# Pooled attention into a two-layer MLP: the output product of four more groups in seven products of quarters, and one set of raw tiles

## The chip, the cores and the metric

The kernel runs on one core of one Trainium2 chip. Its time is the device time of one execution in microseconds (us). The kernel before took 300.4 us, the median of three runs (300.05 to 300.6). Engines are named as the profile names them: PE (matrix products; PEld its weight loads), DVE (vector), ACT (scalar), POOL (GpSimd), SP (here only a queue that issues DMAs).

## The reference

The inputs are q, k, v of shape 8 batches x 8 heads x 576 rows x 64, and two weight matrices, 512 x 2048 and 2048 x 512. The output is 4608 x 512 in float32.

```
k_p = k.reshape(B, H, Sp, 8, D).mean(axis=3)      # 72 pooled keys per head
v_p = v.reshape(B, H, Sp, 8, D).mean(axis=3)
scores = scale * np.matmul(q, k_p.transpose(0, 1, 3, 2))
attn = softmax(scores)                            # over the 72 pooled keys
x = np.matmul(attn, v_p).transpose(0, 2, 1, 3).reshape(B * S, H * D)
h = x @ w_in
g = h - np.tanh(h)
out = g @ w_out
```

## The kernel before, in words

**Groups.** The 4608 tokens are nine groups of 512. Groups 0 to 7 hold the first 512 rows of one batch each; group 8 holds the last 64 rows of all eight batches (the tails, two batches to a unit). A loop over g runs the MLP of group g while it prepares the attention of batch nb = g + 1 and the operands of batch nb + 1 = g + 2. There is no planner: each engine runs its instructions in the order in which the program emits them, and dictionaries (`plan`, `PLAN7`) say after which step of the MLP each step of attention is emitted.

**First product (lines 979 to 998).** `h_mms` makes 128 hidden rows for 512 tokens with 4 matmuls (L426), 64 in all for 16 rows of blocks. For each pair `h_act` runs tanh on ACT (L439) and subtracts on DVE (L440) into `gT`, 16 blocks x 512 tokens in bf16.

**Output product, ordinary (lines 1030 to 1052, groups 1 to 5).** `o_mms` (L483) makes 128 tokens x 512 columns with 16 matmuls, 64 for the group, in 16 steps u.

**Output product, in seven (lines 999 to 1029, groups 6 to 8, `SEVEN`).** A scheme of Winograd's kind with two output column halves, two halves of the 2048 hidden rows and two token halves: seven products (`PRODUCTS`, in the order 4, 2, 7, 1, 6, 5, 3) of 16 matmuls with 256 columns (L561), so 14 steps u and 112 matmuls, and sums round them. `w_sums` (L526) makes four weight sums T1 to T4 once, eight DVE operations. `g_sum` (L543) makes S1 to S4 from quarters of gT in each group: S3 in two halves after steps 13 and 15 of the first product, S2 after u = 2, S1 on POOL behind S2, S4 after u = 8. The products accumulate on top of one another in PSUM banks; `evacuate` copies or subtracts after each (ACT, some DVE), `finish_11` and `finish_22` add the parts on POOL (L593, L594, L598), `store_half` writes the result out.

**Where the sums lie.** T1 to T4 lie in k_raw[0] and v_raw[0], S1 and S2 in q_raw[0], S3 and S4 in q_raw[1], and three partial results n0, n1, p2 in k_raw[1]. So groups 2 to 5, which load batches into both sets of raw tiles, do not use the seven products.

**Attention of batch nb.** Four blocks of 128 rows, and for some groups a tail unit: scores on PE (`s_mms`, L292), row maximum and shift on DVE (L304, L307), exp on ACT (L343), a DMA transpose of E for two blocks at a time (`e_turn_dma`, L352), values on PE (`av_mms`, L379), reciprocal and scaling on DVE (L400, L401), a DMA transpose into xT (`x_turn_dma`, L409), which is what the next group's first product reads.

**Operands.** v of batch nb is pooled on POOL at the start of group g (`pool_v`, L224 to L237). q of batch nb + 1 is cast on ACT behind steps 13 and 15 of the first product (L261) and transposed by DMA; its k is pooled on POOL (`pool_k`, L209 to L215), transposed by DMA (L253) and placed by POOL (L247). Raw tiles exist twice (index b % 2). `load_for(g)` emits the loads of v for batch g + 1 and of q and k for batch g + 2 near the end of a group (u = 13). All these loads, the transposes and the stores are issued from SP, in order; an entry that waits holds back everything behind it.

**Tail values.** In groups of `SEVEN`, the values of a tail unit (`tail_values`) and its transpose are put into `carry` and emitted in the next group after steps 3 and 5 of its first product.

## Time and profile before

| what | value |
|---|---|
| median of three runs | 300.4 us |
| the profiled execution: its own time, and its span | 301.8 us, 300.1 us |
| mean granted PE clock | 0.991 |
| HBM read, written | 36.70 MB, 9.44 MB |
| DVE, tanh subtraction L440 | 64 in all, 1,219 ns each |
| POOL, first step of v's and k's pooling (L224, L209) | 2,908 ns each |
| POOL waiting for v (L224) | 35.7 us in 6 places |
| PE matmul, 512 columns and 256 columns, as recorded | 379 ns and 272 to 273 ns |

Matmuls are pipelined, so their recorded durations overlap; the distance from one to the next is what counts. A row of a timeline is: start in us from the beginning of the span, duration in us, engine, line, operation, what it writes and reads, shapes, how many. In the chain of work a row is start, duration, engine, line and how many. Groups of the kernel are told apart by the times at which the first matmul of L426 starts.

### The profile page before, as it was taken

To read this page: it belongs to the slowest core of one execution; us is meant where nothing else is said; L and a number is where in the kernel's file an instruction comes from. 1 tells how busy PE (TensorE), PEld (TensorE's weight loads), DVE (VectorE), ACT (ScalarE), POOL (GpSimd) and SP (SyncE) were. 2 spreads that over 40 slices of the span, in tenths; PEclk is the share of its full clock that TensorE was granted. 3 is DMA by queue.
4 is the path that set the end of the run, shared out by engine and by line. 5 is a ranking of instruction groups with operands and counts; after the bars stand their busy time and mean duration, and the time that the engine had idled before them with its cause. 6 is when DMAs were issued, how large, how long until landed. Compare 5 with 4: busy or idle time off the path is not lost.

```text
span 300.1 us, 5150 instructions
## 1 busy us (share of the span) xinstructions
PE 286.5 (95%) x2011; PEld 167.5 (56%) x2027; DVE 206.2 (69%) x292; ACT 142.9 (48%) x200; POOL 121.7 (41%) x111
## 2 busy tenths in 40 slices
PE   6799799999999999999999999999999999999993
PEld 2489765444554455445544554455447854784582
DVE  6786484878835993398339932986699947945772
ACT  1786255158504851476137623672376345505620
POOL 7846906029610791098107910791063830010000
PEclk9999799999999999999999999999999999999998
DMA  7999996699988999886889798959823540011005
GB/s 233 225 283 272 205 264 172 129 262 314 228 219 212 332 151 217 239 298 114 204 248 312 137 185 257 328 73 214 232 68 69 103 167 17 2 70 73 0 3 140
DMA packets 84377, 54.55 MB, mean 182 GB/s; under 512 B 58976, under 2 KB 72416, under 8 KB 84352
## 3 DMA queue, kind: packets, MB, share of 16 engines
q1 hardware_dynamic: 77552, 44.90, 57.8%
q0 software_dynamic: 6416, 8.91, 14.3%
q10 hardware_dynamic: 384, 0.39, 0.5%
q8 instruction: 16, 0.26, 0.4%
q14 instruction: 9, 0.07, 0.1%
HBM read 36.70 MB, written 9.44 MB: 154 GB/s over the span
## 4 chain that ended last, share of the span: by engine, by line
PE 77%; DVE 8%; DMA 7%; POOL 3%; ACT 2%; issue 1%; SPq 0%; ACTq 0%; POOLq 0%; DVEq 0%
PE PS L426 32%; PE PS L483 26%; PE PS L561 11%; DMA k_raw<-in_k_dram 4%; PE PS L379 4%; DVE gT L440 3%; DMA q_raw<-in_q_dram 3%; PE PS L292 2%; DVE sh L307 2%; DVE mx L304 2%; PE PS L446 1%; POOL k_raw L209 1%; ACT t_sb L439 1%; PE PS L273 1%; POOL k_raw L212 1%
## 5 line engine op out<-in xcount | busy, mean ns | idle before, releaser
L440 DVE TENSOR_TENSOR gT<-PS,t_sb 128x1024 bf16<-128x1024 f32 x64 | 77.0, 1219 | 40.2 <-ACT t_sb L439 40.2
L426 PE MATMUL PS<-xT,w1b 128*128 128x512 bf16 x448 | 100.8, 379 | 0.0
L483 PE MATMUL PS<-w2b,gT 128*128 128x512 bf16 x368 | 88.7, 379 | 0.8
L439 ACT ACTIVATE t_sb<-PS 128x1024 f32<-128x1024 f32 x64 | 65.5, 1024 | 48.4 <-PE PS L426 47.0
L426 PEld LDWEIGHTS <-w1b 128*128 128x128 bf16 x512 | 49.4, 98 | 55.8
L483 PEld LDWEIGHTS <-gT 128*128 128x128 bf16 x384 | 35.3, 98 | 36.8
L505 ACT COPY o_h<-PS 128x512 f32<-128x512 f32 x22 | 12.8, 583 | 47.7 <-PE PS L483 44.0
L224 POOL TENSOR_TENSOR v_raw<-v_raw 128x1280 f32<-128x1280 f32 x6 | 17.4, 2908 | 35.7 <-DMA v_raw<-in_v_dram 35.7
L343 ACT ACTIVATE E<-sh 128x576 bf16<-128x576 f32 x31 | 21.2, 682 | 15.9 <-DVE sh L307 15.9
L307 DVE TENSOR_TENSOR sh<-PS,mx 128x576 f32<-128x576 f32 x35 | 26.5, 757 | 1.2
L304 DVE TENSOR_REDUCE mx<-PS 128x8 f32<-128x576 f32 x35 | 26.2, 748 | 1.5 <-PE PS L292 1.5
L400 DVE RECIPROCAL rden<-PS 128x8 f32<-128x8 f32 x36 | 7.4, 205 | 25.4 <-PE PS L379 23.4
L401 DVE TENSOR_TENSOR x_sb<-PS,rden 128x512 bf16<-128x512 f32 x32 | 22.1, 692 | 1.1
L561 PEld LDWEIGHTS <-q_raw 128*128 128x128 bf16 x192 | 18.5, 98 | 2.9 <-DVE q_raw L543 0.4
L247 POOL COPY KB<-kT 64x288 bf16<-64x288 bf16 x12 | 5.1, 421 | 35.6 <-DMA kT<-kd 30.2
L209 POOL TENSOR_TENSOR k_raw<-k_raw 128x1280 f32<-128x1280 f32 x6 | 17.4, 2908 | 0.0
L446 PE MATMUL PS<-xT,w1b 128*128 128x128 bf16 x256 | 17.2, 230 | 0.0
L446 PEld LDWEIGHTS <-w1b 128*128 128x128 bf16 x256 | 16.2, 104 | 0.0
L379 PEld LDWEIGHTS <-ET 128*128 128x128 bf16 x192 | 13.1, 98 | 5.2 <-ACT ET L362 0.8
L379 PE MATMUL PS<-VB,ET 128*128 128x130 bf16 (+2 forms) x192 | 15.8, 221 | 0.1
L561 PEld LDWEIGHTS <-gT 128*128 128x128 bf16 x144 | 13.9, 98 | 2.0
L292 PEld LDWEIGHTS <-qT 128*128 128x128 bf16 x128 | 10.0, 98 | 7.6 <-issue 0.8
(99 smaller groups left out, 290.7 us busy)
## 6 DMA issues: line engine op xcount, KB each, us to landing
k_raw<-in_k_dram SPq DMA_DIRECT2D x14, 512.0 KB, 8.6
q_raw<-in_q_dram SPq DMA_DIRECT2D x12, 512.0 KB, 6.9
v_raw<-in_v_dram SPq DMA_DIRECT2D x12, 512.0 KB, 5.1
out_dram<-o_h SPq DMA_DIRECT2D x24, 256.0 KB, 2.5
w1b<-in_moe_w_in_dram POOLq DMA_DIRECT2D x4, 512.0 KB, 9.0
q_raw<-in_q_dram POOLq DMA_DIRECT2D x2, 1024.0 KB, 14.2
w2b<-in_moe_w_out_dram POOLq DMA_DIRECT2D x4, 512.0 KB, 16.4
out_dram<-o_h SPq DMA_DIRECT2D x4, 512.0 KB, 3.3
```

What stands on the lines that cost most here:

```text
L209: eng.tensor_tensor(out=r[:, :, 0:4, :], in0=r[:, :, 0:4, :], in1=r[:, :, 4:8, :], op=ALU.add)
L304: nc.vector.reduce_max(out=mx.rearrange("p k h o -> p k (h o)"), in_=sc, axis=AX.X)
L307: nc.vector.tensor_tensor(out=sh[:, :, :, :], in0=sc, in1=mx.to_broadcast([128, 2, 4, G]), op=ALU.subtract)
L343: nc.scalar.activation(out=E[:, e, :, :].rearrange("p t c -> p (t c)")[:, 0:NK], in_=sh.rearrange("p k h c -> p (k h c)"), func=ACT.Exp, s ...
L379: nc.tensor.matmul(PS[ps, banks[half], D1 * h : D1 * (h + s1 - s0)], lhsT=ET[:, t, c0 : c0 + (ps.stop - ps.start)], rhs=VB[kb][:, t, s0:s1 ...
L401: nc.vector.tensor_tensor(out=x_sb, in0=ps[:, :, :, 0:D], in1=rden.to_broadcast([128, 2, 4, D]), op=ALU.mult,)
L426: nc.tensor.matmul(PS[:, bank, :].rearrange("p (j c) -> p j c", j=R), lhsT=w1b[:, fb, i * 128 : (i + 1) * 128], rhs=xT_of(g)[:, :, fb, :], ...
L439: nc.scalar.activation(out=t_sb[:, :, :], in_=ps, func=ACT.Tanh)
L440: nc.vector.tensor_sub(out=gT[:, i : i + 2, :], in0=ps, in1=t_sb[:, :, :])
L446: mm = nc.tensor.matmul(PS[:, bank, 128 * n : 128 * n + 128], lhsT=w1b[:, fb, (4 * c + n) * 128 : (4 * c + n + 1) * 128], rhs=xT_of(0)[:, ...
L483: mm = nc.tensor.matmul(PS[:, bank, 0 : c1 - c0], lhsT=gT[:, i, tb * 128 : (tb + 1) * 128], rhs=w2b[:, i, c0:c1], start=(i == 0), stop=(i ...
L561: nc.tensor.matmul(ps, lhsT=A[:, i, 128 * b : 128 * b + 128], rhs=B_[:, i, :], start=(n in "24" and i == 0), stop=(i == NQ - 1), skip_grou ...
```

## The change

The seven products are used in groups 2 to 8. T1 to T4 move to k_raw[1] and v_raw[1], S3, n0 and n1 to q_raw[1], p2 to k_raw[1]; S2 gets a tile of its own; S1 overwrites the quarter gT[HI, C2] and S4 the quarter gT[LO, C1]. Batches 2 to 7 use raw set 0 only. In groups of the seven products `pool_k` is emitted right behind `pool_v` at the start of the group, v of batch nb + 1 is loaded right behind the first product, and q's transpose, k's transpose with the tail's load, and the placing of k with the tail's cast and the next loads of q and k are emitted after u = 0, 7 and 13. The carried tail values come after u = 9 and 10 of a group that still has attention. The four weight sums are made in group 1 (their place is "the group before the first of `SEVEN`"). In group 1 v is loaded after u = 0 and 4, k's transpose comes after u = 10 instead of 4, and the stores after u = 4, 11 and 15.

```
-SEVEN = (6, 7, 8)
+SEVEN = (2, 3, 4, 5, 6, 7, 8)
...
+    T1, T2 = quarters(k_raw[1].rearrange("p t n -> p (t n)").bitcast(BF16))
+    T3, T4 = quarters(v_raw[1].rearrange("p t n -> p (t n)").bitcast(BF16))
+    S3 = quarters(q_raw[1].rearrange("p h j d -> p (h j d)").bitcast(BF16))[0]
+    S2 = const.tile([128, NQ, HC], BF16, name="S2")
+    n0, n1 = [
+        q_raw[1][:, h : h + 2, :, :].rearrange("p (b h) j d -> p b (h j d)", b=2) for h in (4, 6)
+    ]
+    p2 = k_raw[1][:, 4, :].rearrange("p (b c) -> p b c", b=2)
+
+    def raw_of(b):
+        return 1 if b == 1 else 0
...
-            1: (S1, a21, a22, ALU.add),
-            2: (S2, a22, S3[:, i, :], ALU.subtract),
-            3: (S3, a11, a21, ALU.subtract),
-            4: (S4, a12, S2[:, i, :], ALU.subtract),
+            1: (a21, a21, a22, ALU.add),
+            2: (S2[:, i, :], a22, S3[:, i, :], ALU.subtract),
+            3: (S3[:, i, :], a11, a21, ALU.subtract),
+            4: (a12, a12, S2[:, i, :], ALU.subtract),
...
-            "3": (S4, 0, w2b[:, LO, C2]),
+            "3": (gT[:, LO, C1], 0, w2b[:, LO, C2]),
...
-            "5": (S1, 0, T1),
+            "5": (gT[:, HI, C2], 0, T1),
...
     def load_for(g):
-        if 1 < g and g + 1 < B:
-            r += v_pieces(g + 1)
...
-    nc.gpsimd.memset(v_raw[1][64:128, 4, :], 0.0)
...
         if nb is not None:
             pool_v(nb, nc.gpsimd)
+        if more and g in SEVEN:
+            pool_k(nb + 1, nc.gpsimd)
         shs = {}
+
+        def seven_more(u):
+            if u == 0:
+                q_turn_dma(nb + 1)
+            if u == 7:
+                k_turn_dma(nb + 1)
+                if nb % 2 == 0:
+                    run(tail_pieces(nb // 2))
+            if u == 13:
+                k_place_kT(nb + 1, ge)
+                if nb % 2 == 0:
+                    tail_cast(nb // 2)
+                load_for(g + 1)
...
-                    if i in (3, 5) and carry:
+                    if nb is None and i in (3, 5) and carry:
                         carry.pop(0)()
...
+        v_next = v_pieces(nb + 1) if more else []
+        if g in SEVEN:
+            run(v_next)
         for u in range(14 if g in SEVEN else 0):
...
+            if nb is not None and u in (9, 10) and carry:
+                carry.pop(0)()
+            if more:
+                seven_more(u)
...
-            if nb is not None and u == 8:
+            if u == (3 if nb is None else 8):
                 g_sum(4, 0, NQ)
...
                 if u == 0:
                     q_turn_dma(nb + 1)
+                    run(v_next, 1)
+                if u == 4:
+                    run(v_next)
                     run(stores)
-                if u == 4:
+                if u == 10:
                     k_turn_dma(nb + 1)
                     k_place_kT(nb + 1, ge)
```

More of the change, by code (lines that the diff above doesn't have):

```diff
@@ L159, in q_pieces @@
             lambda h=h: nc.sync.dma_start(
-                out=q_raw[b % 2][:, h : h + 4, :, :], in_=rows[:, h : h + 4, :, :]
+                out=q_raw[raw_of(b)][:, h : h + 4, :, :], in_=rows[:, h : h + 4, :, :]
             )
@@ L944 @@
             if g in SEVEN:
-                plan = dict(PLAN7)
+                plan = {u: its for u, its in PLAN7.items() if tail is not None or u < 9}
             xs = [x_pair(), x_pair(), x_tl]
@@ L992 @@
                     if i == 15 and nb is None:
-                        for n in (2, 1, 4):
+                        for n in (2, 1):
                             g_sum(n, 0, NQ)
@@ L1033 @@
                 o_store(g, tb, 4 + tb % 2, se)
-                run(stores)
             for it in plan.get(u, ()):
@@ L1048 @@
                     tail_cast(nb // 2)
+            if u in (11, 15):
+                run(stores)
             if u == 13:
```

15 lines of the change are left out of this document (5 added, 10 removed).

## The prediction, made before the result was known

> **What bounds the kernel now.** I read the page's busy times first, then the chain of work that ended last, then PE's instructions in order of time, then DVE and POOL in the one group that already has both attention and the seven products (group 6).
>
> ```profile
> PE 286.5 (95%) x2011; PEld 167.5 (56%) x2027; DVE 206.2 (69%) x292; ACT 142.9 (48%) x200; POOL 121.7 (41%) x111
> ...
> PE 77%; DVE 8%; DMA 7%; POOL 3%; ACT 2%; issue 1%; SPq 0%; ACTq 0%; POOLq 0%; DVEq 0%
> ```
>
> PE is busy nearly throughout and owns 77% of the chain, so a group's price is what stands in PE's queue plus its holes. Group starts on PE (g = 2, 3, 4, 5, 6, 7):
>
> ```profile
> 90.15 4.48 PE L426 MATMUL PS<-xT,w1b 128*128 128x512 bf16 x20
> ...
> 121.45 4.48 PE L426 MATMUL PS<-xT,w1b 128*128 128x512 bf16 x20
> ...
> 151.50 4.48 PE L426 MATMUL PS<-xT,w1b 128*128 128x512 bf16 x20
> ...
> 182.79 4.48 PE L426 MATMUL PS<-xT,w1b 128*128 128x512 bf16 x20
> ...
> 212.84 2.75 PE L426 MATMUL PS<-xT,w1b 128*128 128x512 bf16 x12
> ...
> 242.08 3.62 PE L426 MATMUL PS<-xT,w1b 128*128 128x512 bf16 x16
> ```
>
> Periods: 31.30, 30.05, 31.29, 30.05 us for groups 2 to 5 (2 and 4 carry a tail unit), 29.24 for group 6. The chain's rows give the price of the two kinds of product, 64 wide matmuls (first product, same shape as the ordinary output product) and 112 narrow ones:
>
> ```profile
> 269.18 13.81 PE PS L426 x64
> 282.99 12.38 PE PS L561 x112
> ```
>
> The first bound of an edit in four groups is thus 4 x 1.43 = 5.7 us. What endangers it is seen in group 6. Its DVE has no idle time from 215.87 to 235.3, and PE's third product waits for DVE's sums; then DVE and POOL meet:
>
> ```profile
> 228.16 0.68 DVE L543 TENSOR_TENSOR q_raw<-gT 128x1024 bf16<-128x1024 bf16 x1
> ...
> 231.47 0.69 DVE L543 TENSOR_TENSOR q_raw<-gT 128x1024 bf16<-128x1024 bf16 x1
> ...
> 231.50 2.20 PE L561 MATMUL PS<-v_raw,q_raw 128*128 128x256 bf16 x16
> ...
> 237.40 1.45 DVE L543 TENSOR_TENSOR q_raw<-gT,q_raw 128x2048 bf16<-128x2048 bf16 x1
> ...
> 233.56 4.20 POOL L543 TENSOR_TENSOR q_raw<-gT 128x1024 bf16<-128x1024 bf16 x2 [6.03 <-DVE rden L400]
> 237.72 2.25 POOL L593 TENSOR_TENSOR o_h<-o_h,k_raw 128x512 f32<-128x512 f32 x1
> 240.05 1.27 POOL L594 TENSOR_TENSOR o_h<-o_h,k_raw 128x512 f32<-128x512 f32 x1
> ```
>
> The product at 231.50 takes 2.20 where its neighbours take 1.91: 0.29 us of waiting for the second half of S3, ready at 232.16. The 2048-wide DVE sum at 237.40 takes 1.45 against 1.22 to 1.23 elsewhere while POOL's previous sum ran to 237.76, and POOL's subtraction that starts at 237.72 takes 2.25 where its twin takes 1.27. So a DVE sum of two SBUF tiles and a POOL operation hold each other up.
>
> **The change, part by part.**
>
> *Seven products in groups 2 to 5.* Group 6 is the pattern: 29.24 us with four blocks, a tail's scores, and 0.25 of holes. Groups 2 and 4 become that: -2.06 and -2.05. Groups 3 and 5 lose the tail's scores (0.38) and take the carried tail values of the group before (0.65 in the chain): 29.51, -0.54 each. Sum -5.19 us. The sums add to DVE about 2 x 0.69 + 1.23 + 1.45 + 2 x 0.42 = 4.9 us a group (25.2 busy in group 6's 30 us), to POOL 4.2 + 2.25 + 1.27 + 1.26 = 9.0, to ACT ten copies of 0.37 and one of 0.58 in place of four of 0.58. All that is in group 6's 29.24. What group 6 has not is the next batch's preparation, and that is costed next.
>
> *POOL's pooling of k meets the DVE sums (the term that decides).* POOL's k pooling, 2.91 + 1.54 + 1.54 us, follows v's (7.3 us from first start to the next operation) in its queue now as after; but in groups 2 to 5 DVE has no sum of two SBUF tiles now. With the change the first half of S3 stands at 15.3 us after the group's start, the second at 18.6, S2 at 19.4. When is POOL in k? Group 6's last POOL operation ends 0.46 after the next start; the placing of k's keys (2 x 0.42, 0.90 together) moves behind it: to 1.4. In groups 3 and 5 v's pooling can follow at once, to 8.7, then k must have landed: issued at about 2.5 to 4 behind q and a 0.5 MB store, 2.7 MB at the 0.31 to 0.37 MB/us that the windows from 94 to 104 us show, so about 10.3; its operations run 10.3, 13.2, 14.8 to 16.4 and the sum at 15.3 waits 1.0. In group 4 a tail's cast (landing at 3.0, 0.61) comes first: v to 11.0, k 11.0, 14.0, 15.6: 0.25. In group 2 the same, some 1.5 later, and both halves of S3 are touched: 0.7. DVE has no idle time before S3, so each delay is PE's. Sum 2.95. Bounds: nothing (a sum falls between operations, a delay of POOL alone is hidden; no gain is possible), and a whole 2.91 plus a 1.54 operation in each group, 17.8; the only waits seen, 0.23 and 0.98, are near the value taken.
> The Trainium skill (page "SBUF — State Buffer", section "Who interferes with whom") says that a DVE instruction with two SBUF inputs and a GpSimd instruction that reads SBUF lock each other out for a whole instruction, whoever starts first. The two rows above agree with it. By the rule a sum waits out the whole rest of POOL's operation, as in the 2.95; without it the time would be 300.4 - 5.19 + 0.8 = 296.0.
>
> *v half a group sooner.* Three issues (2 x 0.5 + 0.5 us of SP) go behind the first transpose of E (SP 10.95 to 12.3 after the start, plus 1.3 for the tail's in groups 2 and 4) and in front of the second, and they wait for v's pooling, done at 8.7 to 12.6. POOL's wait for v (3.5 to 11 us in six places) goes, but it is not on the chain; late next is k. v's 1.18 MB run until about 17.5, in tail groups 19. The second transpose is issued at 18.2 in group 6 (231.05), lands 3.5 later, and PE wants it at 234.77: 0.2 spare. Transposes with loads before them landed in 4.3 and 4.5 us (group 2 now), without in 3.3 to 3.5. So nothing in groups 3 and 5, 0.25 in 2 and 4: 0.5 (ends 0 and 4 x 0.85 = 3.4).
>
> *One raw set, order of SP.* q and k of the next batch are issued about 2 us earlier in the group than now (94.07 is 3.9 after 90.15); q lands near 9 and its casts come at 13, so nothing. Those casts, 2 x 1.04 on ACT, are new beside group 6's pattern: tanh, cast, tanh, cast puts the last exp at 230.55 instead of 230.34, covered once DVE is 0.2 late; without that cover 0.2 a group. k's transpose (1.23 to 1.34) goes behind both x transposes: landed 0.2 after the next start, keys placed at 1.4, first scores at 2.6: 1.2 spare. Loads of q and k wait on SP for casts and pooling that ended 10 us before. In-place S1 and S4 lengthen gT's life to the last product; the next write of gT is 3.0 into the next group: nothing.
>
> *T1 to T4 in group 1, not 5.* Eight DVE sums, 0.61 apart, 4.9 us; DVE idles 2.0, 0.96 and 4.6 us between 82.9 and 93.2, POOL's k is done at 80.4: nothing; in group 5 they lay in idle time too and give nothing back. In group 1 three v issues and two stores stand before the x transposes; x lands some 0.7 before group 2: 0.3 (0 to 0.7). The memset of 0.52 was in front of a 3.5 us wait: nothing.
>
> Sum: -5.19 + 2.95 + 0.5 + 0.3 = -1.45 us. The profiled execution took 301.8 (span 300.1, 1.7 around it), so 300.35 on its own footing; against the median of 300.4 it is **298.9**.
>
> **The rivals.**
> *The sums pass POOL (B).* k lands sooner, or POOL always yields: the 2.95 shrinks to 0.4 of casts and small waits; 300.4 - 5.19 + 0.4 + 0.3 = 295.9. For it: POOL has 5 us free a group. Against: 1.45 against 1.23 shows DVE as the one that waits.
> *POOL's long operation stands before the sums (C, the other side).* At L543, first half of S3: if k lands 2.5 us later than I put it, the 2.91 operation starts at 13 and ends near 16, and the second half meets the next one. At 1.6 us a group: 300.4 - 5.19 + 6.4 + 0.8 = 302.4. It decides from an average of 1.2 us a group on. For it: in group 2 now k lands at 105.5, 15 after the start; against: v's 1.18 MB no longer go before it.
> *E's second transpose behind v's load (D).* 0.85 in four groups instead of 0.5 together: 298.9 + 2.9 = 301.8. For: 4.3 to 4.5 us landings with loads in flight; against: v is issued 4 us ahead of it and POOL is ready.
>
> **How the numbers follow.** A (as summed, own range 297.6 to 299.9) 0.45; B 0.20; C 0.22; D 0.13. The measurement tells 0.2% (0.6 us, the spread of three runs) from no change. Faster: A 0.37 + B 0.19 = 0.56; same: 0.08 + 0.01 + 0.03 + 0.04 = 0.16; slower: C 0.19 + D 0.09 = 0.28. The range takes in B and C: 295.6 to 302.5.
>
> **What would show it.** Group periods on PE of 29.9 to 30.5 (2 and 4: 30.2 and 29.5; 3 and 5: 30.5) and S3's first half at over 0.8 us show A. S3 at 0.69 throughout shows B; at over 2 us, or PE's third product at over 3.5, C; PE held before the third block's values by ET, D. T sums all before 91.5 and k's keys placed before the first scores show the parts costed at nothing. Wrong it would be by a wait that I place nowhere: PE on KB or xT at a group's start, ACT on q's casts.

## The result and the profile after

The changed kernel takes 304.98 us (median of four executions, 304.85 to 306.01) against 300.5 for the kernel before on the same chip. The ratio is 1.0149, with a 95% interval of 1.0119 to 1.0179: 1.5% slower, where 298.9 (295.6 to 302.5) had been forecast. The profiled execution, the longest of the four, took 306.01 us (span 304.0, 2.0 around it), 4.2 more than the profiled one of before. 304.98 also lies above the stated range.

The busy times and the chain of work that ended last, on the page of the changed kernel:

```profile
PE 284.0 (93%) x2213; PEld 186.4 (61%) x2219; DVE 228.1 (75%) x316; ACT 149.2 (49%) x228; POOL 157.9 (52%) x130
...
PE 51%; DVE 24%; DMA 10%; POOL 7%; ACT 3%; issue 2%; SPq 0%; DVEq 0%; ACTq 0%; POOLq 0%
```

PE is busy 2.5 us less than before, although this execution holds one stretch more at a low clock (below), and the span is 3.9 us longer. PE's share of the chain falls from 77% to 51%; DVE's triples to 24% and DMA's rises from 7% to 10%. The work became cheaper and the holes between it became larger. The two kinds of product cost what they cost before (rows of the chain in order of time: start, duration, engine, line, how many):

```profile
261.09 12.37 PE PS L567 x112
273.46 13.81 PE PS L432 x64
```

Line numbers have moved by six: L426 is now L432, L561 L567, L543 L549, L409 L415, L352 L358, L209 L215, L526 L532. The starts of groups 2 to 7 on PE's timeline; a bracket at the end of a row is the idle time before the instruction and what ended it:

```profile
92.86 4.01 PE L432 MATMUL PS<-xT,w1b 128*128 128x512 bf16 x12 [2.09 <-DMA xT<-x_sb]
...
125.85 2.75 PE L432 MATMUL PS<-xT,w1b 128*128 128x512 bf16 x12
...
156.72 2.75 PE L432 MATMUL PS<-xT,w1b 128*128 128x512 bf16 x12
...
187.03 2.75 PE L432 MATMUL PS<-xT,w1b 128*128 128x512 bf16 x12
...
217.03 2.75 PE L432 MATMUL PS<-xT,w1b 128*128 128x512 bf16 x12
...
246.36 3.62 PE L432 MATMUL PS<-xT,w1b 128*128 128x512 bf16 x16
```

The start of group 1 lies between 56.3 and 59.0 us in the profiled executions of this study, also where nothing ahead of it differs, so kernels are compared by the periods between these starts. (It is 58.5 to 59.0 in the four executions, before and changed among them, whose clock falls in group 0, and 56.3 to 57.4 in the other twelve.) The forecast by group, put together from its terms, against what the two profiles show:

| group | before | after | forecast change | measured change |
|---|---|---|---|---|
| 1 | 31.63 | 33.89 | +0.30 | +2.26 |
| 2 | 31.30 | 32.99 | -1.11 | +1.69 |
| 3 | 30.05 | 30.87 | +0.46 | +0.82 |
| 4 | 31.29 | 30.31 | -1.55 | -0.98 |
| 5 | 30.05 | 30.00 | +0.46 | -0.05 |

The five rows sum to -1.44 forecast and +3.74 measured; what is left of the 4.2 is a later start of group 1 (+0.45), the groups behind (-0.29) and the time around the span (+0.3). Groups 3 to 5 together came out 0.42 above the forecast. The loss is in groups 1 and 2: 4.76 us above it. All this holds for the two profiled executions; no other execution of these two kernels has a profile.

**Group 1.** PE waits 2.09 us for x at 92.86. These are SP's rows ahead of it in the changed kernel:

```profile
83.85 0.57 SPq L137 DMA_DIRECT2D v_raw<-in_v_dram  x1
84.48 0.48 SPq L143 DMA_DIRECT2D v_raw<-in_v_dram  x1
85.00 1.06 SPq L514 DMA_DIRECT2D out_dram<-o_h  x2
86.15 4.58 SPq L415 DMA_TRANSPOSE xT<-x_sb  x2
```

and in the kernel before:

```profile
83.98 1.01 SPq L508 DMA_DIRECT2D out_dram<-o_h  x2
85.08 2.88 SPq L409 DMA_TRANSPOSE xT<-x_sb  x2
```

The first x transpose is issued 1.07 us later (0.62 counted from the start of the group). The two issues then take 4.58 us instead of 2.88, and they land 5.7 and 4.4 us after their issue instead of 3.2 and 2.7. The chain of work that ended last has the second one:

```profile
87.15 1.17 DVE v_raw L532 x2
88.32 4.40 DMA xT<-x_sb
```

Counted from the start of the group the second transpose is issued 1.14 us later and lands 1.7 slower; some 0.7 was to spare, and 2.1 is left as PE's wait. The lateness is in the issuing and the landing more than in the place in the order. The chain names two of the weight sums (L532) just before that issue, but they are not the cause: in e2 below no weight sum stands in group 1, and PE waits there too.

**The clock behind that wait.** The granted clock in two stretches after 92.86 (busy us and instructions of PE, PEld, DVE, ACT and POOL, then the granted clock as a share of full speed, DMA share, GB/s):

```profile
94.00:98.00 4.00, 4.00 (x15) 1.74 (x14) 1.70 (x2) 1.02 (x1) 1.39 (x4) 0.57 1.02 280
98.00:102.00 4.00, 4.00 (x23) 1.96 (x22) 2.90 (x4) 2.62 (x3) 3.92 (x2) 1.00 0.89 259
```

The mean clock is 0.57 for 4 us, and 15 matmuls run where 23 run in the next 4 us. Group 2's first product takes 16.49 us (92.86 to 109.35) where it takes 14.81 elsewhere (group 2 of e8_kpool_split, below): 1.7 us on top of the 2.09. The three other executions of the changed kernel have a mean clock of 0.994 against this one's 0.986, and 302.8 to 303.1 us of span against 304.0; whether they hold this stretch is not on record. The Trainium skill (page "TensorE: Matmul & The Clock Gate", section "What's actually happening") says that an idle window of about 3.4 us halves PE's clock. The trace agrees with the size of the step (0.50 from 95 to 97 us), but the wait ahead of it was 2.09 us, and waits of 1.02 to 1.68 at the same place (e2, e3, e4, e8, e9 and e15 below) left the matmuls behind them at full speed. The length of a wait alone does not decide it. In group 0, where PE waits for POOL in every run, the matmuls behind waits of 1.92 (e4), 2.22 (before), 2.48 (e1) and 2.60 us (changed kernel) ran at half clock, and those behind waits of 2.17 to 2.72 in seven other runs at full clock. What else decides is open.

**Group 2.** PE also waits 0.77 for S3's second half and 1.25 for ET, what E's second transpose writes:

```profile
114.56 1.48 PE L567 MATMUL PS<-v_raw,q_raw 128*128 128x256 bf16 x12 [0.77 <-DVE q_raw L549]
...
118.52 0.53 PE L385 MATMUL PS<-VB,ET 128*128 128x130 bf16 x6 [1.25 <-DMA ET<-E]
```

**Groups 3 to 5.** DVE and POOL meet at the sums, as forecast. Group 3, first DVE, then PE, then POOL, on their timelines:

```profile
141.26 1.96 DVE L549 TENSOR_TENSOR q_raw<-gT 128x1024 bf16<-128x1024 bf16 x1
...
144.82 0.52 PE L385 MATMUL PS<-VB,ET 128*128 128x130 bf16 x6 [0.51 <-DVE sh L313]
...
146.59 1.48 PE L567 MATMUL PS<-v_raw,q_raw 128*128 128x256 bf16 x12 [0.82 <-DVE q_raw L549]
...
138.14 2.91 POOL L215 TENSOR_TENSOR k_raw<-k_raw 128x1280 f32<-128x1280 f32 x1 [3.86 <-DMA k_raw<-in_k_dram]
141.12 1.54 POOL L218 TENSOR_TENSOR k_raw<-k_raw 128x640 f32<-128x640 f32 x1
142.74 1.87 POOL L221 TENSOR_TENSOR kd<-k_raw 128x640 bf16<-128x640 f32 x1
```

S3's first half takes 1.96 us against 0.68 alone. It starts 0.14 after a POOL operation that runs from 141.12 to 142.66 and ends at 143.22, 0.56 after that one: it waited it out. POOL's next operation, begun at 142.74 while the sum ran, takes 1.87 instead of 1.54. PE pays 0.51 and 0.82.

### The profile page after: what moved, and what is told of

Same layout as the page of the kernel before. It is cut to its first block, busy times and chain, and to the rows that moved or that the text cites. A ratio compares the mean times of both kernels' runs of the same rounds, so it can differ in the third digit from the quotient of the medians.

```text
span 304.0 us, 5609 instructions
## 1 busy us (share of the span) xinstructions
PE 284.0 (93%) x2213; PEld 186.4 (61%) x2219; DVE 228.1 (75%) x316; ACT 149.2 (49%) x228; POOL 157.9 (52%) x130
## 4 chain that ended last, share of the span: by engine, by line
PE 51%; DVE 24%; DMA 10%; POOL 7%; ACT 3%; issue 2%; SPq 0%; DVEq 0%; ACTq 0%; POOLq 0%
PE PS L567 20%; PE PS L432 19%; DVE gT L446 12%; PE PS L489 6%; DVE sh L313 5%; DVE mx L310 4%; DMA k_raw<-in_k_dram 4%; PE PS L385 3%; DMA q_raw<-in_q_dram 3%; DVE q_raw L549 3%; DMA ET<-E 2%; DMA xT<-x_sb 1%; PE PS L452 1%; ACT t_sb L445 1%; PE PS L298 1%
## 5 line engine op out<-in xcount | busy, mean ns | idle before, releaser
L432 PE MATMUL PS<-xT,w1b 128*128 128x512 bf16 x448 | 102.3, 383 | 2.1 <-DMA xT<-x_sb 2.1
L432 PEld LDWEIGHTS <-w1b 128*128 128x128 bf16 x512 | 49.7, 99 | 58.1 <-issue 3.9
L567 PEld LDWEIGHTS <-gT 128*128 128x128 bf16 x560 | 53.5, 98 | 6.8
L567 PE MATMUL PS<-w2b,gT 128*128 128x256 bf16 x336 | 40.9, 273 | 0.0
L549 POOL TENSOR_TENSOR gT<-gT 128x1024 bf16<-128x1024 bf16 x10 | 21.0, 2119 | 20.7 <-DVE rden L406 20.7
L489 PE MATMUL PS<-w2b,gT 128*128 128x512 bf16 x122 | 30.1, 379 | 0.3
L215 POOL TENSOR_TENSOR k_raw<-k_raw 128x1280 f32<-128x1280 f32 x6 | 17.4, 2907 | 13.7 <-DMA k_raw<-in_k_dram 13.6
L594 DVE TENSOR_TENSOR o_h<-PS,q_raw 128x256 f32<-128x256 f32 x22 | 9.3, 424 | 16.2 <-PE PS L567 16.2
L600 POOL TENSOR_TENSOR o_h<-o_h,k_raw 128x512 f32<-128x512 f32 x6 | 8.5, 1412 | 22.3 <-DVE o_h L594 21.9
L385 PE MATMUL PS<-VB,ET 128*128 128x130 bf16 (+2 forms) x192 | 16.5, 221 | 2.1 <-DMA ET<-E 1.2
L489 PEld LDWEIGHTS <-gT 128*128 128x128 bf16 x128 | 11.6, 98 | 10.9
L567 PE MATMUL PS<-v_raw,q_raw 128*128 128x256 bf16 x112 | 14.2, 273 | 3.2 <-DVE q_raw L549 3.2
```

The lines of the kernel that those rows point to most:

```text
L385: nc.tensor.matmul(PS[ps, banks[half], D1 * h : D1 * (h + s1 - s0)], lhsT=ET[:, t, c0 : c0 + (ps.stop - ps.start)], rhs=VB[kb][:, t, s0:s1 ...
L432: nc.tensor.matmul(PS[:, bank, :].rearrange("p (j c) -> p j c", j=R), lhsT=w1b[:, fb, i * 128 : (i + 1) * 128], rhs=xT_of(g)[:, :, fb, :], ...
L489: mm = nc.tensor.matmul(PS[:, bank, 0 : c1 - c0], lhsT=gT[:, i, tb * 128 : (tb + 1) * 128], rhs=w2b[:, i, c0:c1], start=(i == 0), stop=(i ...
L549: return eng.tensor_tensor(out=o, in0=x, in1=y, op=op)
L567: nc.tensor.matmul(ps, lhsT=A[:, i, 128 * b : 128 * b + 128], rhs=B_[:, i, :], start=(n in "24" and i == 0), stop=(i == NQ - 1), skip_grou ...
```

## The experiments

The theory after this comparison: three separate costs stand on the path. They are x behind v and the stores in group 1, DVE's sums behind POOL's pooling of k, and a late second transpose of E in group 2. The rivals were that the raw set or the new order costs something everywhere, and that any one of them is paid back elsewhere when it is taken away. In the texts put on record before the first runs, theory 1 is the first of these accounts, theory 2 has all of the loss in the meeting of DVE and POOL, and theory 3 in loads that wait for the one raw set.

### Which part of the change costs

**One raw set alone (e11).** The old order of SP and the ordinary output product in groups 2 to 5; what stays is one raw set for batches 2 to 7.

```
-SEVEN = (2, 3, 4, 5, 6, 7, 8)
+SEVEN = (6, 7, 8)
...
                 o_store(g, tb, 4 + tb % 2, se)
+                run(stores)
...
                 if u == 0:
                     q_turn_dma(nb + 1)
-                    run(v_next, 1)
+                    run(stores)
                 if u == 4:
-                    run(v_next)
-                    run(stores)
-                if u == 10:
                     k_turn_dma(nb + 1)
                     k_place_kT(nb + 1, ge)
...
-            if u in (11, 15):
-                run(stores)
             if u == 13:
+                run(v_next)
                 load_for(g + 1)
```

> One raw set and the sums in set 1 alone: ordinary output product in groups 2 to 5, and SP's order as in the kernel before (v at u = 13 in front of q and k, k's transpose at u = 4, stores as before). Theory 1 (a load into the one raw set never waits, only the places of v and the stores in SP's queue cost): 300.3 within 0.5, no wait of PE for x or ET. Theory 3 (the raw set holds the loads): 302 or more, as in the run with the changed order (305.48), with waits for ET in groups 2 to 5.

Measured: 300.60 us, ratio 0.9995 (0.997 to 1.002); periods of groups 1 to 5 of 31.64, 31.29, 30.05, 31.29 and 30.06, those of before to 0.01. One raw set costs nothing.

**The rest of the change without the seven products in groups 2 to 5 (e2).** Only the set is undone, so v stays half a group sooner and the stores behind it.

```
-SEVEN = (2, 3, 4, 5, 6, 7, 8)
+SEVEN = (6, 7, 8)
```

> The changed kernel with the ordinary output product in groups 2 to 5 again (seven products in 6 to 8 only); one raw set, v sooner and the order of SP stay. Theory 1: only group 1's loss is left, so 300.4 + 2.3 to 3.9 = 302.7 to 304.3, the wait of PE for x at group 2's start is still there, and groups 2 to 5 take 31.3, 30.05, 31.3, 30.05. Theory 2: 300.2 to 300.8. Theory 3: 304 or more, with waits of PE for x or ET in each of groups 2 to 5.

Measured: 305.48 us, ratio 1.0175 (1.0138 to 1.0213). Here the order that the change gives group 1 holds for groups 1 to 5. PE waits 1.35 for x at 90.37, and in groups 2 to 5 it waits 0.76, 0.52, 0.21 and 1.07 for ET, with v and stores ahead of E's second transpose. Since one raw set costs nothing (e11), the order of SP is dear by itself: with group 1's order throughout and without the products the kernel is as slow as the changed one. (The changed kernel has another order in its groups 2 to 5.)

**The products without POOL's pooling of k (e3).** The pooling of k in groups 2 to 5 is left out.

```
-        if more and g in SEVEN:
-            pool_k(nb + 1, nc.gpsimd)
```

> The changed kernel without the pooling of k on POOL in groups 2 to 5 (k's pooled rows of an earlier batch are used again, so a part of the computation is left out). Loads, transposes and all sums stay. Theory 1: S3's first half takes 0.69 in each group in place of 1.08, 1.96, 1.66 and about 1.4, PE's wait for S3 falls to the 0.2 to 0.3 of group 6, and 2.5 to 3.3 us go: 301.7 to 302.5; the wait for x stays. Theory 2: back to 299.5 or less. If the sums are late for another reason (ACT's two casts in front of the last exp, gT late), S3 is early but PE waits as before: 304 or more.

Measured: 299.55 us, ratio 0.9973 (0.9942 to 1.0003). Groups 3, 4 and 5 take 29.60, 29.32 and 29.60. S3's halves take 0.68 and 0.69, PE's wait for S3 is 0.20 in each of these groups, and the waits for x (1.45 at 90.50) and for ET in group 2 (1.75) stay. What the meeting costs in groups 3 to 5 is thus 91.18 - 88.52 = 2.66 us, and in group 2 the 0.77 us of waiting, 3.4 together. The time is near the 299.5 that theory 2 gave, 5.4 below the changed kernel's median, but theory 2 is not shown by it: the waits for x and ET are on the path here too. For the 2 us beyond 3.4 this profile offers two differences that are not the meeting: it has no low clock in group 2, and its wait for x, ahead of the edit, is 0.64 shorter.

**Short operations on POOL (e8).** The same pooling in fifteen operations, one fifth each, instead of three.

```
-            pool_k(nb + 1, nc.gpsimd)
+            for t in range(NT):
+                pool_k(nb + 1, nc.gpsimd, t, t + 1)
```

> The changed kernel with k's pooling on POOL in groups 2 to 5 in fifteen operations of a fifth (one row block of 512, 256, 256 numbers) instead of three. If a DVE sum of two SBUF tiles waits for the end of the POOL operation that is running, it now waits at most one short operation at a time: S3's first half 0.7 to 1.4 instead of up to 1.96, PE's wait for S3 0.3 to 0.6 instead of 0.8, 1 to 2 us less: 303.0 to 304.0. If the two engines share the bandwidth over the time they overlap, S3 is as slow as before: 304.6 to 305.4.

Measured: 300.39 us, 4.6 below the changed kernel's median and more of a gain than the 1 to 2 us expected; ratio 0.9961 (0.9936 to 0.9986). Groups 3 to 5 take 29.60, 29.62 and 29.67. The first halves of S3 in groups 2 to 5, from DVE's timeline:

```profile
105.70 0.88 DVE L549 TENSOR_TENSOR q_raw<-gT 128x1024 bf16<-128x1024 bf16 x1
...
137.19 0.68 DVE L549 TENSOR_TENSOR q_raw<-gT 128x1024 bf16<-128x1024 bf16 x1
...
166.79 0.98 DVE L549 TENSOR_TENSOR q_raw<-gT 128x1024 bf16<-128x1024 bf16 x1
...
196.41 0.75 DVE L549 TENSOR_TENSOR q_raw<-gT 128x1024 bf16<-128x1024 bf16 x1
```

The longest is 0.98 us, where it was 1.96. The work on POOL is the same and its operations still lie beside the sums. Only their length changed, and groups 3 to 5 came to within 0.4 us of the run without pooling: what a sum pays is the rest of the POOL operation that it finds under way. In groups 3 to 5 that is 2.3 us (91.18 to 88.89). This execution also had no stretch at the low clock in group 2, so not all of the 4.6 us need be the pooling; the waits for x (1.68) and for ET in group 2 (1.79) are still there.

**k ahead of q (e4).** If k lands earlier, the pooling is over before the sums.

```
-            r += q_pieces(g + 2) + k_pieces(g + 2)
+            r += k_pieces(g + 2) + q_pieces(g + 2)
```

> The changed kernel with k loaded before q in every group's end (two k issues and a small one in front of two q issues). Theory 1: k lands some 3 us sooner; POOL waited 3.9 and 2.3 us for k in groups 3 and 4, so k's pooling ends about when S3's first half is made in 3 and 5, and only v's pooling in front of it sets it in 2 and 4: 1.5 to 2.5 us less, 302.5 to 303.5. If q, which then lands 3 us later, holds ACT's casts (13 us after the start), 305 or more. If DVE and POOL do not matter: 304.98 within 0.5.

Measured: 302.71 us, ratio 1.0062 (1.0033 to 1.0091). Groups 3 to 5 take 29.66, 29.95 and 29.60, nearly those without pooling. In group 3 POOL starts k at 135.46 after a wait of 1.03 instead of 3.86, and S3's first half takes 0.74. Group 1 pays 1.26 more than in the changed kernel (35.15): PE waits 0.72 for DVE at 78.25 and 0.83 for ACT at 83.81. With q behind k there, ACT's cast waits 1.83 for q and holds up the tanh behind it.

### Group 1

**The old place of stores and v in group 1 (e1).**

```
                 if u == 0:
                     q_turn_dma(nb + 1)
-                    run(v_next, 1)
-                if u == 4:
-                    run(v_next)
                     run(stores)
...
             if u == 13:
+                run(v_next)
                 load_for(g + 1)
```

> The changed kernel, except that in group 1 the two old stores go to SP behind q's transpose (u = 0) and the three loads of v go behind both x transposes, in front of the next q and k (u = 13), as before the change. Theory 1 (two separate losses: the x transposes of group 1 land late behind v and stores, and DVE's sums meet POOL's k pooling): the 2.1 us wait of PE at the start of group 2 goes, with what the lower PE clock costs behind it in the profiled execution (1.7 us): 304.98 - 2.3 to -3.9 = 301.1 to 302.7. Theory 2 (all of it is the meeting of DVE and POOL in groups 2 to 5, and group 1's wait is taken up by it): 304.5 or more. Theory 3 (loads into the one raw set hold SP): within 0.5 of 304.98, with a new wait elsewhere.

Measured: 306.51 us, ratio 1.0204 (1.016 to 1.0248). The x wait is gone and group 1 takes 31.64, but the 301.1 to 302.7 of theory 1 did not come: group 2 takes 35.43. v of batch 3 is issued at 94.87, and POOL waits 6.70 us for it, so that its pooling of k lies on top of all three sums. DVE, POOL and PE in group 2:

```profile
109.53 3.35 DVE L549 TENSOR_TENSOR q_raw<-gT 128x1024 bf16<-128x1024 bf16 x1
112.92 2.44 DVE L549 TENSOR_TENSOR S<-gT,q_raw 128x2048 bf16<-128x2048 bf16 x1
...
109.45 2.88 POOL L215 TENSOR_TENSOR k_raw<-k_raw 128x1280 f32<-128x1280 f32 x1
112.41 1.86 POOL L218 TENSOR_TENSOR k_raw<-k_raw 128x640 f32<-128x640 f32 x1
...
110.51 0.53 PE L385 MATMUL PS<-VB,ET 128*128 128x130 bf16 x6 [1.63 <-DMA ET<-E]
112.94 2.74 PE L567 MATMUL PS<-v_raw,q_raw 128*128 128x256 bf16 x12 [1.46 <-DVE q_raw L549]
```

A sum of 0.68 that starts 0.08 after a POOL operation of 2.88 takes 3.35 us. This is the clearest row of the whole-instruction lock that the prediction took from the Trainium skill (page "SBUF — State Buffer", section "Who interferes with whom"), and the trace agrees.

**v of group 1 right behind the x transposes (e6).** Stores after step 0 as in the run before, v after step 10 behind the x and k transposes, new stores only after step 15.

```
                 if u == 0:
                     q_turn_dma(nb + 1)
-                    run(v_next, 1)
-                if u == 4:
-                    run(v_next)
                     run(stores)
                 if u == 10:
                     k_turn_dma(nb + 1)
                     k_place_kT(nb + 1, ge)
+                    run(v_next)
...
-            if u in (11, 15):
+            if u == 15:
                 run(stores)
```

> The changed kernel, group 1 only: old stores behind q's transpose (u = 0), v's three loads behind both x transposes and k's transpose (u = 10), new stores all at u = 15, behind the next q and k. Theory 1, amended after putting v at u = 13 moved the loss into group 2: what counts in group 1 is that x goes before v and that v, q and k still go out early, because group 2's pooling of v holds k's pooling, its own v loads and with them SP's second transpose of E. So group 1 takes 31.6 to 31.9 (33.89 now), group 2 29.9 to 31 (32.99 now), PE waits neither for x nor more than 0.5 for ET in group 2: 300.0 to 301.5. If v loads in front of the second transpose of E are the cause by themselves, group 2 keeps its wait of 1.2 to 1.7 for ET: 301.5 to 302.7. If only DVE and POOL matter: 304 or more.

Measured: 304.92 us, ratio 1.0112 (1.0056 to 1.0168). Group 1 takes 31.64 again, and group 2 36.05, where 29.9 to 31 had been expected. Its wait is now in the queue:

```profile
108.40 0.53 PE L385 MATMUL PS<-VB,ET 128*128 128x130 bf16 x6 [0.90 <-DMA ET<-E]
...
116.12 0.59 PE L385 MATMUL PS<-VB,ET 128*128 128x130 bf16 x6 [4.09 <-DMA ET<-E]
```

The first E transpose is issued at 100.90 behind the q and k loads and four stores and lands 7.5 us later. v of batch 4 is issued only at 106.69, and the second transpose stands behind it and lands 7.3 us after its issue. The time is that of the account in which only DVE and POOL matter (304 or more), but the waits are for ET.

**The two edits together (e7): k ahead of q, and group 1 as in the last run (not shown again).**

```
-            r += q_pieces(g + 2) + k_pieces(g + 2)
+            r += k_pieces(g + 2) + q_pieces(g + 2)
```

> The same group 1 and k loaded before q everywhere. Theory 1: the two repairs add up, since they touch different groups: 1.5 to 2.5 less than the run with group 1 alone, groups 3 to 5 at 29.6 to 30.0, 298.0 to 299.5, faster than the kernel before (300.3). If the repairs overlap (group 2 is all there is): no better than group 1 alone within 0.5.

Measured: 304.97 us, ratio 1.012 (1.006 to 1.0181). Groups 3 to 5 take 29.59, 29.66 and 29.60, but group 1 is 35.41 (2.01 of waiting for DVE at 78.04) and group 2 35.66 (4.51 for ET at 119.37). Groups 3 to 5 gain 1.1 us on e6, and group 1 loses 3.8, three times what k ahead of q cost it in e4 (1.26). The two repairs do not add up.

### The second transpose of E in group 2

**v behind the transpose (e9).** v of the next batch is loaded after step 8 of the output product in groups 2 to 7, behind E's second transpose.

```
             if u == 7:
                 k_turn_dma(nb + 1)
...
+            if u == 8:
+                run(v_next)
...
-        if g in SEVEN:
-            run(v_next)
```

> The changed kernel with one move: in groups 2 to 7 the three loads of v are issued after step 8 of the output product, behind the second transpose of E, instead of ahead of it. Theory: v in the queue is what makes group 2's second transpose land late (5.3 us, 1.25 us of PE waiting for ET at 118.52); that wait goes and groups 3 to 5 stay as they are (30.87, 30.31, 30.00), so group 2 falls from 32.99 to about 31.7 and the time from 305.0 to about 303.7. Rival: the load that is moved only moves its price: v lands after the next group's start, POOL's pooling of k comes 1 us or more later and the sums of S3 and S2 meet it in groups 3 to 5 for longer (periods 31 and more); the time stays at 305 or rises.

Measured: 304.31 us, ratio 1.0102 (1.0054 to 1.0151); the four executions took 302.89, 303.88, 304.74 and 307.94. Three of them lie round the expected 303.7, but by luck: the wait that was to go stays, and in this profile group 1 is 1.07 us shorter than in the changed kernel's (32.82), with no low clock behind it. So the theory falls. No load stands ahead of the transpose now, and it still lands 5.2 us after its issue; PE still waits 1.10. Group 2's 32.66 hold two more waits, 1.04 for the shift of the scores at 109.43 and 1.06 for S3 at 111.44; the periods of groups 3 to 5 (31.00, 30.56, 29.86) hardly moved. DMA throughput in 40 equal slices from 110 to 115.3 us (the transpose is issued at 110.03), with the instruction queue's line from the same view (packets, MB, share of 16 engines' time):

```profile
GB/s 0 0 0 0 0 0 0 0 0 100 213 213 222 207 209 205 216 218 160 124 153 201 259 255 222 215 106 66 0 0 0 0 4 8 10 10 10 10 153 298
...
q8 instruction: 1, 0.02, 1.1%
```

The queue is empty until 111.2, then transposes run at some 210 GB/s. At 113.7 the traffic stops for 0.5 us, goes on at 4 to 10 GB/s until 115.0, and at 115.25 PE's wait ends. In these 5.3 us one packet of 0.02 MB of instructions was fetched. It starts to count between 113.31 and 113.38, and its 1.1% of 16 engines' time is some 0.9 us of one engine, so it ends at about 114.2, where the 4 to 10 GB/s begin. The reading that fits is that one of the sixteen DMA engines fetched the packet first and moved its share of the transpose last (a sixteenth of 210 GB/s would be 13). No view shows the engines one by one. The Trainium skill (page "DMA: Bandwidth & Descriptors", section "Why a DMA increments its semaphore by 16 and not by 1") says that a transfer has landed when the last of its engines has finished; the tail of 1.3 us, 0.8 of it at 4 to 10 GB/s, agrees. The changed kernel's own trace has the same tail in group 2 (113.1 to 118.5):

```profile
GB/s 349 152 46 30 46 15 46 30 15 89 212 212 218 209 205 214 220 212 142 148 144 209 262 224 188 216 116 28 38 0 0 0 4 8 9 9 9 9 119 294
...
q8 instruction: 1, 0.02, 1.1%
```

The kernel before has it too, in its group 2 (110 to 114.5 us; the transpose is issued at 110.07, with no load under way):

```profile
GB/s 225 203 187 207 199 46 0 0 146 0 0 112 198 200 207 196 171 61 9 0 7 9 9 9 9 9 14 223 289 282 291 289 285 274 291 282 291 287 67 0
...
q8 instruction: 1, 0.02, 1.9%
```

This transpose lands in 4.3 us, those of groups 3 to 5, on which no packet falls, in 3.4 to 3.5. PE did not need it sooner there. It is one of the two landings, 4.3 and 4.5, that the prediction put down to loads in front.

**Moving the fetch (e15).** This is e8_kpool_split with PE's instruction stream 56 pairs longer at the very start.

```
-    fill(11, 7)
+    fill(2, 7)
+    fill(65, 7, 64)
```

> As e8_kpool_split, with PE's instruction stream longer by 56 pairs of weight load and matmul before its first real work: in the warm-up at the start 11 matmuls of zeros with 512 columns become 2 of these and 65 with 64 columns, about as long together; nothing else is changed. Theory (a packet of code is fetched by one of the DMA engines while group 2's second transpose of E runs; that engine's share comes last and PE waits 1.79 us for ET): the fetch falls some 5 us earlier against the work, the transpose lands in 3.3 to 3.7 us instead of 5.6, the ET wait of group 2 goes, its period falls from 31.41 to 29.6 to 30.1 and the time from 300.4 to about 298.8. Rival (v's load and the stores in front of the transpose make it late): the wait and the period stay, and the time stays at 300.4.

Measured: 300.68 us, ratio 0.9984 (0.9961 to 1.0006): no gain in time, so the expected 298.8 failed and the time is near the rival's 300.4. The fetches did move, by 6.5 us against the work in group 2 (from 22.0 to 15.4 us after its start) and by 4.3 in group 4 (from 25.7 to 21.4). In group 4 a fetch now falls on E's second transpose, which it had not done in e8. Throughput there, from 169.7 to 175 us, in e15:

```profile
GB/s 402 433 340 124 16 0 0 0 0 102 207 218 218 205 214 199 218 214 174 191 186 217 356 224 207 162 46 0 0 0 2 8 8 10 10 10 10 128 284 290
...
q8 instruction: 1, 0.02, 1.4%
```

and in e8, from 169.9 to 175.2:

```profile
GB/s 464 325 448 464 294 480 402 140 15 33 199 214 207 211 201 218 218 214 195 158 193 217 253 234 222 213 222 201 214 214 216 222 224 213 224 211 220 151 207 188
```

The tail came with the fetch: the transpose lands in 5.1 us instead of 3.4, and PE waits 0.72 for ET in group 4, where it had waited nothing. In group 2 the wait fell from 1.79 to 1.11 and did not go. The fetch now meets the load of v (issued at 105.22; its last piece lands at 112.6), and the transpose, issued at 108.65 behind it, has the same stop at 111.6 to 112.4 (0 to 22 GB/s) without a packet of instructions in its own time, and lands in 5.1 us. So in group 4 the fetch alone makes the wait, and in group 2 a load ahead of the transpose can make nearly the same one, as the rival has it. In the changed kernel the load was almost done when the transpose was issued (15 to 46 GB/s from 113.4 to 114.3), and its tail is the fetch's.

### Taking the costs away together

**Split pooling, group 1 as in e6 (not shown again), v of group 2 behind its second transpose (e12).**

```
-            pool_k(nb + 1, nc.gpsimd)
+            for t in range(NT):
+                pool_k(nb + 1, nc.gpsimd, t, t + 1)
...
+            if u == 8:
+                run(v_next)
...
-        if g in SEVEN:
+        if g in SEVEN and g > 2:
             run(v_next)
```

> The changed kernel with three edits for the three costs named: the pooling of k in groups 2 to 5 as fifteen POOL operations of one fifth instead of three (the meeting with the sums); in group 1 the stores of the group before after step 0 and v after step 10, behind the x transposes (the x wait); and in group 2 alone v after step 8, behind the second transpose of E (the ET wait). Theory (three separate costs, each on the path): group 1 31.6, group 2 30.0 to 30.5, groups 3 to 5 29.6 to 29.7, so 296.6 to 297.5, faster than both. Rival (the queue only shifts its load): with v late in group 1, v of batch 3 and of batch 4 and group 2's transposes still stand in one queue; group 2 stays at 31.5 or more and the time at 298.5 or above.

Measured: 302.63 us, ratio 1.0047 (1.0018 to 1.0076), slower than the split alone. Groups 1, 3, 4 and 5 are nearly as forecast (31.64, 29.98, 29.55, 29.59), and group 2 takes 36.58. The rival's numbers came out, but the longest wait is in a place that neither account named. PE and POOL:

```profile
117.45 1.04 PE L567 MATMUL PS<-k_raw,gT 128*128 128x256 bf16 x4 [2.01 <-POOL gT L549]
119.52 2.74 PE L567 MATMUL PS<-k_raw,gT 128*128 128x256 bf16 x12 [1.04 <-POOL gT L549]
...
114.24 5.22 POOL L549 TENSOR_TENSOR gT<-gT 128x1024 bf16<-128x1024 bf16 x2
```

The tail's rows, which POOL casts first and whose load stands behind v's in the queue, land late (POOL waits 5.72 us for them), so POOL begins v's pooling 8.2 us after the group's start instead of 4.8. It ends k's at 114.2, and S1, which POOL makes behind it, holds PE's sixth product for 3.05 us. The following twelve and sixteen matmuls take 2.74 and 2.95 instead of 1.48 and 1.91, at a granted clock of 0.50.

**The same with v late in all groups (e13).**

```
-        if g in SEVEN and g > 2:
-            run(v_next)
```

> As the run before it, but v after step 8 in groups 2 to 7 and not in group 2 alone. Theory: in groups 3 to 6 v ahead of the second transpose costs nothing (no ET wait there), so the periods of groups 3 to 6 are the same within 0.1 us and the time within 0.5 us of the run before. Rival: v half a group sooner does help groups 3 to 5 (POOL gets to k sooner): then S3's first half is longer here and the time 0.5 to 2 us above the run before.

Measured: 308.35 us, ratio 1.029 (1.0212 to 1.0368). Groups 3 and 5 are within 0.4 of the run before (29.62, 29.75), but group 4 takes 34.55, with 3.3 us of PE waiting for S1, because POOL waited 4.32 us for v after that group's start. So v half a group sooner is not a detail of the change: where v comes late, S1 comes late.

**S1 of group 2 on DVE (e14).** As e12, with one more edit.

```
+                if g == 2:
+                    after([g_sum(1, 0, NQ)], dep)
+                else:
                     after([g_sum(1, 0, 4, nc.gpsimd), g_sum(1, 4, NQ, nc.gpsimd)], dep)
```

> As e12_split_and_order, but in group 2 the sum S1 is made by DVE, as one operation behind S2, instead of by POOL behind its pooling. Theory (with v late, POOL ends its pooling at 114.2 and S1, which PE's sixth product reads, stands behind it; DVE has 7.0 us idle in that group): the 3.05 us of PE waiting for gT go and group 2 falls from 36.58 to 31 to 32.5, the other groups stay within 0.2; the time falls from 302.6 to 297 to 298.5. Rival (DVE is the next one late): S1 ahead of the scaling of x holds up the x transposes and DVE's 1.2 us meets POOL's short operations; group 2 stays above 34 and the time above 300.5.

Measured: 299.31 us, ratio 0.9936 (0.9904 to 0.9968), by the ratio 0.6% faster than the kernel before, and above the 297 to 298.5 expected. Group 2 falls from 36.58 to 31.32 and the wait for S1 in it is gone. Left in group 2 are 0.62 for ET at 107.71 and 1.19 for the scaling of x at 112.63 (S1 stands in front of it on DVE). Group 3 is worse than expected at 31.05: its v, which group 2 loads late, keeps POOL waiting for 2.87 us, and PE waits 1.35 for that group's S1. The ten executions spread from 296.7 to 301.8.

**The last two additions together (e17).** e14 with the longer PE stream of e15.

```
-    fill(11, 7)
+    fill(2, 7)
+    fill(65, 7, 64)
```

> Both of the runs before it together: v late in groups 1 and 2, pooling in fifths, S1 of group 2 on DVE, and PE's stream 56 pairs longer. If the three costs (x wait, S1 behind POOL, code fetch beside the transpose) are separate: group 1 31.64, group 2 29.7 to 30.5, groups 3 to 5 29.6 each, time 296 to 297.3, below both kernels. If the queue in front of group 2's transposes holds them anyway (landings of 4.9 us and more with v of batch 3 issued at 87 to 90): ET wait of 1 us or more in group 2, time 297.5 to 298.5.

Measured: 299.54 us, ratio 0.9965 (0.994 to 0.999). All groups but the first are above what was expected. Group 2 takes 30.96, and group 4 takes 31.10 where e14 had 29.32, with 0.89 of waiting for ET and 0.91 for S3. As in e15, a fetch now falls on group 4's second transpose: the wait was moved, not taken away.

## Why the prediction was wrong, by its own steps

**"Seven products in groups 2 to 5", -5.19: right.** It gave 29.51, 29.24 and 29.51 for groups 3 to 5 without the meeting. Without the pooling (e3) they take 29.60, 29.32 and 29.60, each with 0.20 of waiting.

**"POOL's pooling of k meets the DVE sums", +2.95: right in mechanism and nearly in size.** e3 puts it at about 3.4; PE's waits that belong to it in the changed kernel are 0.77, 1.33, 1.03 and 0.60 us in groups 2 to 5, 3.73 in sum, of which 0.20 in each of groups 3 to 5 stands without the pooling too. The spread was off: k's pooling begins 14.6 (group 2) and 12.3 us (group 3) after the group's start, because k lands later than the 10.3 estimated. In group 4 it begins at 12.0 instead of 11.0, and the group pays 1.03 and not 0.25. By its wide bounds (0 to 17.8) the step could have been anywhere; the two waits it had seen, 0.23 and 0.98, chose well. With the spread wrong, the near sum is in part luck.

**"Three v issues and two stores stand before the x transposes", +0.3 (0 to 0.7): the step that failed.** It set what stands before the transposes against the 0.7 that x had to spare, and gave no price to the landing. The issue was only 1.07 us later. But v's load and the stores were still moving, the two x transposes took 1.70 us more to issue, and the second needed 4.40 us to land instead of 2.7. Group 1 lost 2.26 us, in this execution; the other profiled executions with this order in group 1 wait 1.02 to 1.68 there. The wait of 2.09 was then followed by the low clock, 1.7 us more, for which the prediction had no term. The trace of before had a row for that, which the prediction did not read. In group 0 PE waited 2.22, and its next 32 matmuls of 128 columns took 3.42. But that row gives no price by itself: the same 32 take 1.95 behind a longer wait in e6. First the kernel before, then e6 (PE's timelines):

```profile
31.98 0.66 PE L273 MATMUL PS<-ident,kd 128*128 128x128 bf16 x5 [2.22 <-POOL kd L215]
32.43 3.42 PE L446 MATMUL PS<-xT,w1b 128*128 128x128 bf16 x32
...
32.48 0.45 PE L279 MATMUL PS<-ident,kd 128*128 128x128 bf16 x5 [2.72 <-POOL kd L221]
32.77 1.95 PE L452 MATMUL PS<-xT,w1b 128*128 128x128 bf16 x32
```

The prediction's closing sentence, that it would be wrong "by a wait that I place nowhere: PE on KB or xT at a group's start", named the place, but gave it no chance.

**"v half a group sooner", +0.25 in group 2: too small, and for another reason than rival D's.** PE waited 1.25 for ET in group 2 and nothing in groups 3 to 5. D put it on v ahead of the transpose. e9 moved v away and left 1.10, and the throughput shows the tail that comes with a packet of instructions. D's reason is real where the load is late (e15, group 2). Of the two landings that spoke for D, the 4.3 had no load in front of it but a packet (above). No step of the prediction looked at where PE's code is fetched, although the change lengthens PE's stream by some 400 instructions and so shifts every fetch against the work.

**"One raw set", nothing: right** (e11, ratio 0.9995). "k's transpose and keys", nothing: right, no wait for KB stands in the changed kernel's groups. "T1 to T4 in group 1", nothing: right, e1, e6, e12 and e14 take 31.64 in group 1 with these sums in it, and the kernel before 31.63 without them.

**The rivals.** The side came out as in C, but not by C: POOL's long operation cost 0.9 us a group, below the 1.2 that it needed. The order that the prediction itself put at 0.8 us (0.3 + 0.5) decided: x and ET cost 3.5 us by the periods and waits, and the low clock 1.7.

The sum by measured terms: groups 1 and 2 lost 4.76 us more than forecast. Of these 2.0 are x's wait beyond the 0.3, 1.7 the clock behind it in the profiled execution, and 1.0 the wait for ET beyond 0.25. Two ends stay open. The order's 3.5 us are read from periods and waits: every edit that took the wait for x away paid for it in group 2 or 3 (e1, e6, e12, e14), and the most that came back is 1.1 us (e14 against e8). And the medians of e3 and e8 lie 2 us lower than the meeting alone explains; the low clock and the length of the x wait differ between executions, and the other executions have no profile.

## What to carry to other kernels

A DMA that is moved behind others is late by more than the issues it is moved past: price its landing with those transfers still moving. After a wait of PE of about 2 us, look also at the clock behind it: it may fall, and it may not. When two engines hold each other up for whole instructions, cut the instruction that is off the path into short ones: the same pooling in fifths gave back nearly all of what leaving it out would give. Before an engine with slack is given a new duty, follow its queue to the last entry: POOL had time enough for k's pooling, but S1 stood behind it, and where an edit made POOL late by several us (e12, e13, e14) PE paid there.

## What the runs showed of the hardware that was not expected

- A packet of 0.02 MB of instructions fetched beside a DMA transpose made it land in 4.3 us (kernel before, group 2) to 5.3 us (changed kernel) instead of 3.4 to 3.5, with about 1 us at 0 to 10 GB/s inside it. Lengthening PE's stream by 56 pairs at the start moved the packets against the work and brought this wait to another group (0 to 0.72 us in group 4).
- A wait of PE of 2.09 us was followed by 4 us at a mean granted clock of 0.57 (changed kernel), and waits of 2.01 and 1.04 with four matmuls between by sixteen matmuls in 2.95 us instead of 1.91 (e12). But at one place in group 0 the clock fell behind waits of 1.92 to 2.60 us in four profiled executions and stayed at 1.00 behind 2.17 to 2.72 in seven others. Where it fell there, group 1 started at 58.5 to 59.0 us instead of 56.3 to 57.4.
- A DVE sum of 0.68 us took 3.35 where it started 0.08 after a POOL operation of 2.88 (e1). The same pooling in fifths left sums of at most 0.98 (e8).
- With the queue full, a transpose behind loads and stores took 2.91 us to issue and 7.5 to land (e6), against 1.34 and 3.4.
